# Linear attention and a GELU layer on one core: keys and values cut into 512 main tokens and 64 rest tokens, in place of nine tokens to a partition

## The chip, the core and the metric

The kernel runs on one core of one Trainium2 chip. TensorE (PE) multiplies matrices and writes to PSUM, eight banks of 2 KB per partition. VectorE (DVE), ScalarE (ACT) and GpSimd (POOL) do the elementwise work in SBUF, which has 128 partitions; DVE and ACT also read PSUM. SyncE (SP) only issues transfers (DMA); ACT issues some as well. Each engine takes its instructions in order, and they wait for one another through semaphores.

The metric is the time of one execution in microseconds (us), as the median of several. In the profile, L380 is line 380 of the kernel, and `out<-in` names the tiles that an instruction writes and reads.

## The reference

Eight batches of eight heads, 576 tokens (S) and 64 channels (D) go through linear attention with the feature map phi(x) = elu(x) + 1. The heads are put side by side to 512 channels, and a two-layer network follows: 512 to 2048 (`w_in`), GELU in its tanh form, 2048 to 512 (`w_out`). All is float32 in HBM.

```python
phi = lambda x: np.where(x > 0, x, np.exp(x) - 1.0) + 1.0
q_p, k_p = phi(q), phi(k)                            # q, k, v: (8, 8, 576, 64)
kv  = np.einsum('bhsd,bhse->bhde', k_p, v)           # 64 x 64 for each batch and head
z   = np.sum(k_p, axis=2)
num = np.einsum('bhsd,bhde->bhse', q_p, kv)
den = np.einsum('bhsd,bhd->bhs', q_p, z)[..., None] + 1e-06
x = (num / den).transpose(0, 2, 1, 3).reshape(8 * 576, 512)
h = x @ w_in                                         # (4608, 2048)
g = 0.5 * h * (1.0 + np.tanh(np.sqrt(2 / np.pi) * (h + 0.044715 * h**3)))
out = g @ w_out                                      # (4608, 512)
```

## The kernel before

**Feature map.** phi is computed as min(exp(x), max(x + 1, 1)). ACT takes the exponential (`exp_of`, L212), DVE takes max(x + 1, 1) (`linear_of`, L220) and then the minimum (`least_of`, L228). The results are bf16 (`q_p`, `k_p`).

**Queries.** Of each batch, tokens 0 to 511 (`MAIN`) are loaded with four tokens to a partition and all eight heads side by side (`load_q`, L99). The last 64 tokens (`REST`) of two batches share one tile of 128 partitions, `qr` (`load_rest`, L110). The minimum of q is transposed by four DMA transposes on SP's queue to `qt`, channels on the partitions (`least_q`, L597).

**Keys and values.** The 576 tokens of a head are 64 partitions of nine tokens each (J = 9), so two neighbouring heads, which lie one behind the other in HBM, fill 128 partitions: `load_pairs` (L90) reads runs of 2304 bytes, and four pairs of heads (`u`) make a tile. `v` is cast to bf16 into `vp`, which has a 65th column of ones for each head (E = 65), so that one product gives both kv and z.

**The kv products** (`kv_paired`, L242). For each of nine token slots, a pair of heads `u = 2 * ii + s` and a member `a` of the pair, a matmul contracts 64 partitions: the array is used as four quarters of 64x64. Row half `a` is the head within the pair, column half `s` the pair. A batch takes 9 x 2 x 2 x 2 = 72 matmuls of 64 columns by 65. The results go into block-diagonal tiles `kvbds` (a head pair in two 64x65 blocks, 128x130 in all) for batches 0 to 3, or compact tiles `kvs` for batches 4 to 7.

**The n products**, q_p times kv with the denominator as 65th column. For batches 0 to 3, `nab` (L311) and its kin use the block-diagonal tile: per 128 tokens four matmuls of 128x128 by 130 columns. For batches 4 to 7, `n_quads` (L276) uses quarters of 64x64: 16 matmuls by 65 columns per 128 tokens. `divide` (L289) is a reciprocal and a multiplication on DVE, which give `x`. `x` is transposed to `xt` by a DMA transpose on SP's queue (`transposed_x`, L621); for batches 0 and 1 PE transposes.

**The network.** `iteration(j)` (L741) runs the two large products for batch j's 512 tokens; iteration 8 does the rest tokens of all eight batches (`xt_rest`). It has 16 steps h (four matmuls of 512 columns each; ACT applies GELU into `g`) and 16 steps o (four matmuls each; four tiles t of 128 tokens by four ranges of m). From iteration 2 on all h come first (slots 0 to 15), then o by tiles (slots 16 to 31). Evictions of o alternate between DVE and ACT, and ACT issues the stores.

**The order by hand.** The schedule is manual. `at(j, slot, fn)` puts a piece of attention work for a later batch behind a slot of iteration j; work of one slot runs in the order in which it was registered. This order is also that of every queue, SP's among them:
- `plan_prepare(b, ...)` (L575): the maps of batch b and its cast of v; for b from 4 on in iteration b - 2 at slots 13 to 19.
- `plan_by_chunks` (L628): kv and the four chunks of n for batches 2 (iteration 1, slots 16 to 24) and 3 (iteration 2, slots 2 to 10).
- `plan_attention(b, m_rest)` (L636): for batches 4 to 7, in iteration b - 1, an early block at slot 5 (two chunks of n and the rest of two batches) and a late one at slot 22 (two chunks, kv of batch b + 1, the minimum and the transposes of q of batch b + 1).
- `load_batch` (L118): q, k and v of a batch on SP's queue; batch 2 before the first matmul of the network, batch 4 in iteration 1 at slot 29, 5 in iteration 2 at slot 23, 6 and 7 in iterations 3 and 4 at slot 6. k and q of batch 3 come with batch 2, its v and the first rest of q in iteration 1 at slot 10.

**Storage.** Loads go to seven buffers of one pool (`pld`), rests of q to two (`pqr`). In PSUM, six single banks rotate among h, o and the small products (`ps_b`), and one pair of banks (`ps_a`, `pair_of_banks`) serves n and kv.

**Batches 0 and 1** have their own paths (`first_batch`, `plan_second`) with PE transposes. SP loads them first, together with the weights, which DVE, ACT and POOL cast to bf16.

**The last tile** (`last_tile`, L733) of iteration 8 is computed in three pieces of columns; ACT copies the first, DVE the other two (L738).

Of the kernel before, what the change touches and what calls it, by code (L numbers as in the profile page):

```python
# [15 lines left out]
def kernel(  # L16
# [33 lines left out]
    pld = ctx.enter_context(tc.tile_pool(name="pld", bufs=7))  # L50
    pqr = ctx.enter_context(tc.tile_pool(name="pqr", bufs=2))
# [32 lines left out]
    ld = {}  # L84

    def ld_tile(name, b):
        shape = [P, H, C * D] if name == "q" else [P, NP, J * D]
        ld[name, b] = pld.tile(shape, FP32, name=name + "_x", tag="ld")
# [10 lines left out]
    def load_q(b):  # L99
        ld_tile("q", b)  # L100
        nc.sync.dma_start(
            out=ld["q", b],
            in_=q[b, :, 0:MAIN, :].rearrange("h (p c) d -> p h (c d)", c=C),
        )

    def load_all_pairs(name, src, b):
        ld_tile(name, b)
        load_pairs(name, src, b)

    def load_rest(m):  # L110
        t = ld["qr", m] = pqr.tile([P, H, D], FP32, name="qr")
        for s in range(2):
            nc.sync.dma_start(
                out=t[REST * s : REST * (s + 1)],
                in_=q[2 * m + s, :, MAIN:S, :].rearrange("h p d -> p h d"),
            )

    def load_batch(b):  # L118
        load_q(b)
        load_all_pairs("k", k, b)  # L120
        load_all_pairs("v", v, b)
# [53 lines left out]
    load_q(3)  # L175
    load_all_pairs("k", k, 3)
# [6 lines left out]
    vps = [pkv.tile([P, J * NP, E], BF16, name=f"vp{i}") for i in range(2)]  # L183
    kvbds = [pkv.tile([P, NP, 2 * E], BF16, name=f"kvbd{i}") for i in range(4)]
    kvs = [pkv.tile([P, NP, E], BF16, name=f"kv{i}") for i in range(4)]
    for i in range(2):
        nc.gpsimd.memset(vps[i][:, :, D:E], 1.0)
    for t in kvbds:
        nc.gpsimd.memset(t, 0.0)

    def vp_paired(b):
        return vps[b % 2].rearrange("p (j u) e -> p j u e", u=NP)

# [4 lines left out]
    def maps_view(name, b, x, out, hs):  # L198


        i = x[:, hs].rearrange("p h (c d) -> p h c d", d=D)
        o = out[:, :, hs, :].rearrange("p c h d -> p h c d")
        if name == "qr" or (name == "q" and b > 1):
            i = i.rearrange("p (u a) c d -> p a u c d", a=2)
            o = o.rearrange("p (a u) c d -> p a u c d", a=2)
        return o, i
# [5 lines left out]
    def exp_of(name, b, hs=None):  # L212
        x = ld[name, b]
        hs = hs or slice(0, x.shape[1])
        if (name, b) not in exps:
            exps[name, b] = pe.tile([P, x.shape[2] // D, x.shape[1], D], BF16, name=name + "_e")
        o, i = maps_view(name, b, x, exps[name, b], hs)
        nc.scalar.activation(o, i, AF.Exp)  # L218

    def linear_of(name, b, hs=None):  # L220
        x = ld[name, b]
        hs = hs or slice(0, x.shape[1])
        if (name, b) not in phi:
            phi_tiles(name, b)
        o, i = maps_view(name, b, x, phi[name, b], hs)
        nc.vector.tensor_scalar(o, i, 1.0, 1.0, op0=ALU.add, op1=ALU.max)  # L226
# [9 lines left out]
    def cast_v_paired(b, us, fn):  # L236
# [3 lines left out]
        )  # L240

# [14 lines left out]

    def kv_evac(b, blocks, src, fn):
        for s in range(2):
            r = slice(HP * s, HP * (s + 1))
            fn(out=kvbds[b][r, blocks, E * s : E * (s + 1)], in_=src[r])  # L260

    def nab_mm(qt_c, kvbd, ns):
        for i in range(NP):
            nc.tensor.matmul(  # L264
                ns[i // 2][:, 2 * E * (i % 2) : 2 * E * (i % 2 + 1)],
                lhsT=qt_c[:, i, :],
# [4 lines left out]
    def kv_of_head(b, s, i):  # L271

        r = slice(HP * s, HP * (s + 1))
        return kvs[b % 4][r, i, :] if b > 3 else kvbds[b][r, i, E * s : E * (s + 1)]

    def n_quads(qt_c, bs, ns):  # L276

        for i in range(NP):
            for t in range(2):
                for s in range(2):  # L280
                    c = slice(HP * t, HP * (t + 1))
                    nc.tensor.matmul(  # L282
                        ns[s][c, E * i : E * (i + 1)],
                        lhsT=qt_c[HP * s : HP * (s + 1), i, c],
                        rhs=kv_of_head(bs[t], s, i),
                        skip_group_check=True,
                    )

    def divide(x_v, n_v):  # L289

        heads = tuple(slice(None) for _ in n_v.shape[:-1])
        shape = list(n_v.shape[:-1])
        r = psm.tile(shape, FP32, name="r" + "".join(str(d) for d in shape[1:]))
        nc.vector.reciprocal(r, n_v[heads + (D,)])  # L294
        nc.vector.tensor_tensor(  # L295
            x_v,
            n_v[heads + (slice(0, D),)],
            r[heads + (None,)].to_broadcast(shape + [D]),
            op=ALU.mult,
        )  # L300

    def x_tile():
        return px.tile([P, d_model], BF16, name="x")

    def by_parity(x):
        return x.rearrange("p (u a d) -> p a u d", a=2, d=D)

    def by_half(x):
        return x.rearrange("p (i s a d) -> p s a i d", s=2, a=2, d=D)

    def nab(qt_c, b):  # L311
        x, n_ps = x_tile(), pair_of_banks("n_ps")
        nab_mm(qt_c, kvbds[b], [n_ps[:, a] for a in range(2)])
        divide(by_parity(x), n_ps[:, :, 0 : 4 * E].rearrange("p a (u e) -> p a u e", e=E))
        return x

    def nab_in_banks(qt_c, b):
        x, ns = x_tile(), [bank("n_ps", [P, 4 * E]) for _ in range(2)]
        nab_mm(qt_c, kvbds[b], ns)
        for a in range(2):  # L320
            divide(by_parity(x)[:, a], ns[a].rearrange("p (u e) -> p u e", e=E))
        return x

    def nab_quads(qt_c, bs):

        n_ps = pair_of_banks("n_ps")
        n_quads(qt_c, bs, [n_ps[:, s] for s in range(2)])

        def x_of():
            x = x_tile()  # L330
            n_v = n_ps[:, :, 0 : NP * E].rearrange("p s (a i e) -> p s a i e", a=2, e=E)
            divide(by_half(x), n_v)
            return x

        return x_of

    def nab_quads_in_banks(qt_c, bs):
        ns = [bank("n_ps", [P, NP * E]) for _ in range(2)]
        n_quads(qt_c, bs, ns)

        def x_of():
            x = x_tile()
            for s in range(2):
                divide(by_half(x)[:, s], ns[s].rearrange("p (a i e) -> p a i e", a=2, e=E))
            return x

        return x_of
# [59 lines left out]
    def first_batch():  # L407
# [50 lines left out]
        x = {0: x_tile()}  # L458
# [116 lines left out]
    def plan_prepare(b, s_linear, s_exp):  # L575
        def casts():
            cast_v_paired(b, slice(0, NP), nc.vector.tensor_copy)

        order = "qk" if b < 5 else "kq"

        def exps_all():
            for n in order:
                exp_of(n, b)

        j, s = s_linear
        for i, n in enumerate(order):
            at(j, s + i, linear_of, n, b)
# [3 lines left out]
        if b < 5:  # L591
            at(j, s + 2, least_q, b)
            at(j, s + 4, least_of, "k", b)
        else:
            at(j, s + 2, least_of, "k", b)

    def least_q(b):  # L597
        least_of("q", b)
        qts[b] = pt.tile([P, C, NP, P], BF16, name="qt")
        for c in range(C):  # L600
            nc.sync.dma_start_transpose(
                out=qts[b][:, c],
                in_=phi["q", b][:, c].rearrange("p h d -> p (h d)"),
            )

    def kv_in_pair(b):
        kv_ps = pair_of_banks("kv_ps")
        for ii in range(2):
            kv_paired(b, ii, lambda a, ii: kv_ps[:, a, E * ii : E * (ii + 1)])
        src = kv_ps[:, :, 0 : 2 * E].rearrange("p a (i e) -> p a i e", e=E)  # L610
        if b > 3:
            nc.vector.tensor_copy(out=kvs[b % 4].rearrange("p (a i) e -> p a i e", a=2), in_=src)
        else:
            for s in range(2):
                r = slice(HP * s, HP * (s + 1))
                nc.vector.tensor_copy(
                    out=kvbds[b][r, :, E * s : E * (s + 1)].rearrange("p (a i) e -> p a i e", a=2),
                    in_=src[r],
                )

    def transposed_x(b, c, x):  # L621
        if b not in xts:
            xts[b] = pt.tile([P, NP, MAIN], BF16, name="xt")
        nc.sync.dma_start_transpose(out=xt_chunk(b, c), in_=x)

    rest_qt = {}

    def plan_by_chunks(b, j, s_kv, s_n):  # L628
        def n(c):
            transposed_x(b, c, nab(qts[b][:, c], b))  # L630

        at(j, s_kv, kv_in_pair, b)
        for c in range(C):
            at(j, s_n + 2 * c, n, c)

    def plan_attention(b, m_rest):  # L636


        j = b - 1

        def pair_of_chunks(c):
# [193 lines left out]
```

## Time and profile before

| What | Value |
|---|---|
| Three runs | 287.03, 286.35, 285.89 us; median 286.35 |
| The profiled execution's own time | 287.03 us |
| Its span, first to last instruction | 285.2 us |
| Granted clock of TensorE | 1.00 |
| Large matmuls of 512 columns, L725 and L380 | 560 + 492 + 64, 379 ns each, starts 0.216 us apart |
| kv matmuls L248, 64 rows x 64 columns x 65 | 576, busy 6.6 us |
| n matmuls L264, 128 x 128 x 130 | 60, busy 5.8 us |
| n matmuls L282, 64 x 64 x 65 | 256 + 64, busy 4.9 us |
| Loads of k and v, 1152 KB each | median 10.8 and 11.8 us from issue to landing |
| Loads of q, 1024 KB each | 6.4 us |
| Loads of rests of q, 128 KB each | 9.0 us |
| DMA transposes of x | 24, 3.7 us |

Matmuls are pipelined: one of 512 columns is shown with 379 ns, but the next starts 216 ns after it, so the time of a stretch is read from starts, or from the chain of waits, and not from a sum of durations. Time of an engine other than PE counts only where PE waits for it. The chain of waits names, in order of time, the instructions that followed one another up to the end of the execution.

### The profile page before, as it was taken

The page shows a single profiled execution, that of the slowest core. Times are in us where ns is not written, and L with a number is a line of the kernel's source. Part 1 is how long each engine was busy: PE and PEld are TensorE (multiplying, and loading weights), DVE is VectorE, ACT ScalarE, POOL GpSimd, SP SyncE. Part 2 cuts the span into 40 slices and gives each one's busy share as a digit, 9 for nine tenths or more (in the row PEclk, how much of TensorE's full clock was granted, in tenths as well). Part 3 has the DMA queues.
Part 4 walks back from the last instruction along what each step waited for, and adds up shares of the span by engine and source line. Part 5 has one row for each costly group of instructions (what it writes and reads, how often), then busy time and mean ns, then how long its engine had stood idle before and what let it go on. Part 6 is the DMA issues. An engine that isn't in the chain of part 4 may idle for free.

```text
span 285.2 us, 5408 instructions
## 1 busy us (share of the span) xinstructions
PE 278.3 (98%) x2298; PEld 135.7 (48%) x2298; DVE 106.8 (37%) x192; ACT 161.2 (57%) x222; POOL 19.0 (7%) x24
## 2 busy tenths in 40 slices
PE   7999999999989999999999999999999999999995
PEld 3484455445445444445444544454444444444444
DVE  2850396434865550727072815372403000000001
ACT  4768876795966844684368626771650165026400
POOL 4147251000000000000000000000000000000000
PEclk9999999999999999999999999999999999999999
DMA  6999999926998958999828953006310610120022
GB/s 232 400 406 397 411 401 403 404 60 194 160 223 285 289 147 259 332 339 307 168 45 301 302 164 79 19 21 175 103 37 1 121 65 0 49 90 11 0 74 75
DMA packets 59575, 53.83 MB, mean 189 GB/s; under 512 B 35744, under 2 KB 45344, under 8 KB 59552
## 3 DMA queue, kind: packets, MB, share of 16 engines
q1 hardware_dynamic: 56768, 44.57, 52.2%
q10 hardware_dynamic: 2784, 8.91, 9.0%
q8 instruction: 18, 0.29, 0.4%
q14 instruction: 5, 0.04, 0.1%
HBM read 36.70 MB, written 9.44 MB: 162 GB/s over the span
## 4 chain that ended last, share of the span: by engine, by line
PE 82%; DMA 10%; DVE 3%; SPq 2%; issue 1%; POOL 1%; DVEq 0%
PE h_ps L380 39%; PE o_ps L725 39%; DMA w_st<-in_moe_w_in_dram 5%; DMA k_x<-in_k_dram 4%; PE kv_ps L248 2%; PE n_ps L282 1%; SPq L129 1%; PE n_ps L264 1%; DMA xt<-x 1%; SPq L92 1%; DVE k_p L232 1%; POOL w_in_sb L141 1%; DVE vp L237 1%; DVE q_p L232 0%; DVE q_p L226 0%
## 5 line engine op out<-in xcount | busy, mean ns | idle before, releaser
L725 PE MATMUL o_ps<-w_out_sb,g 128*128 128x512 bf16 (+2 forms) x608 | 127.9, 368 | 0.0
L380 PE MATMUL h_ps<-xt,w_in_sb 128*128 128x512 bf16 (+1 forms) x564 | 115.4, 360 | 0.7 <-DMA xt<-x 0.7
L390 ACT ACTIVATE g<-h_ps 128x512 bf16<-128x512 f32 x144 | 84.9, 599 | 42.0 <-PE h_ps L380 41.1
L380 PEld LDWEIGHTS <-w_in_sb 128*128 128x128 bf16 x628 | 57.8, 98 | 63.7 <-issue 1.4
L725 PEld LDWEIGHTS <-g 128*128 128x128 bf16 x608 | 57.6, 98 | 64.1
L686 ACT COPY o_sb<-o_ps 128x512 f32<-128x512 f32 (+1 forms) x19 | 10.8, 575 | 65.0 <-PE o_ps L725 64.1
L686 DVE COPY o_sb<-o_ps 128x512 f32<-128x512 f32 (+1 forms) x19 | 12.3, 647 | 73.5 <-PE o_ps L725 73.5
L295 DVE TENSOR_TENSOR x<-n_ps,r 128x256 bf16<-128x256 f32 (+1 forms) x49 | 26.4, 539 | 1.7
L294 DVE RECIPROCAL r<-n_ps 128x4 f32<-128x4 f32 (+1 forms) x49 | 9.2, 187 | 39.8 <-PE n_ps L282 30.1
L232 DVE TENSOR_TENSOR k_p<-k_p,k_e 128x2304 bf16<-128x2304 bf16 (+1 forms) x9 | 11.9, 1317 | 18.9 <-ACT k_e L218 18.8
L218 ACT ACTIVATE k_e<-k_x 128x2304 bf16<-128x2304 f32 (+1 forms) x9 | 17.1, 1904 | 0.9 <-DMA k_x<-in_k_dram 0.8
L218 ACT ACTIVATE q_e<-q_x 128x2048 bf16<-128x2048 f32 (+1 forms) x9 | 15.4, 1716 | 3.3 <-DMA q_x<-in_q_dram 3.2
L226 DVE TENSOR_SCALAR q_p<-q_x 128x2048 bf16<-128x2048 f32 (+1 forms) x9 | 9.9, 1103 | 13.7 <-DMA q_x<-in_q_dram 13.6
L380 PE MATMUL h_ps<-xt_rest,w_in_sb 128*128 128x512 bf16 x64 | 14.0, 379 | 0.0
L226 DVE TENSOR_SCALAR k_p<-k_x 128x2304 bf16<-128x2304 f32 (+1 forms) x9 | 11.0, 1222 | 6.2 <-DMA k_x<-in_k_dram 6.2
L232 DVE TENSOR_TENSOR q_p<-q_p,q_e 128x2048 bf16<-128x2048 bf16 (+1 forms) x9 | 9.9, 1101 | 7.3 <-ACT q_e L218 7.2
L237 DVE CAST vp<-v_x 128x2304 bf16<-128x2304 f32 (+1 forms) x9 | 11.4, 1266 | 2.3 <-DMA v_x<-in_v_dram 2.2
L412 PE MATMUL w_ps<-warm 128*128 128x512 bf16 x37 | 10.1, 423 | 1.2 <-DVE warm L181 1.2
L403 ACT ACT_TABLE_LOAD x8 | 10.3, 1283 | 0.1
L218 ACT ACT_TABLE_LOAD x7 | 9.0, 1283 | 0.1
L141 POOL CAST w_in_sb<-w_st 128x512 bf16<-128x512 f32 (+2 forms) x6 | 7.6, 1269 | 14.8 <-DMA w_st<-in_moe_w_in_dram 14.8
L147 POOL CAST w_out_sb<-w_st 128x2048 bf16<-128x2048 f32 (+2 forms) x5 | 7.1, 1427 | 8.7 <-DMA w_st<-in_moe_w_out_dram 8.7
(47 smaller groups left out, 76.8 us busy)
## 6 DMA issues: line engine op xcount, KB each, us to landing
out_dram<-o_sb ACTq DMA_DIRECT2D x16, 512.0 KB, 3.5
k_x<-in_k_dram SPq DMA_DIRECT2D x7, 1152.0 KB, 10.8
v_x<-in_v_dram SPq DMA_DIRECT2D x7, 1152.0 KB, 11.8
q_x<-in_q_dram SPq DMA_DIRECT2D x6, 1024.0 KB, 6.4
w_st<-in_moe_w_in_dram SPq DMA_DIRECT2D x3, 1024.0 KB, 13.6
w_st<-in_moe_w_out_dram SPq DMA_DIRECT2D x3, 1024.0 KB, 12.4
q_x<-in_q_dram SPq DMA_DIRECT2D x4, 512.0 KB, 8.5
k_x<-in_k_dram SPq DMA_DIRECT2D x2, 576.0 KB, 6.1
```

What stands on the lines that cost most here:

```text
L141: fn(out=w_in_sb[:, :, 512 * i + fs.start : 512 * i + fs.stop], in_=w_st[True, i][:, :, fs],)
L218: nc.scalar.activation(o, i, AF.Exp)
L226: nc.vector.tensor_scalar(o, i, 1.0, 1.0, op0=ALU.add, op1=ALU.max)
L232: nc.vector.tensor_tensor(p, p, e, op=ALU.min)
L237: fn(out=vp_paired(b)[:, :, us, 0:D].rearrange("p j u d -> p u j d"), in_=ld["v", b][:, us].rearrange("p u (j d) -> p u j d", d=D),)
L295: nc.vector.tensor_tensor(x_v, n_v[heads + (slice(0, D),)], r[heads + (None,)].to_broadcast(shape + [D]), op=ALU.mult,)
L380: nc.tensor.matmul(h_ps[:, ts], lhsT=w_in_sb[:, c, P * m : P * (m + 1)], rhs=xt[:, c, ts], start=(c == 0), stop=(c == KM - 1), skip_group_ ...
L390: nc.scalar.activation(g[:, m, :], h_ps, AF.Gelu_apprx_tanh)
L403: nc.scalar.preload_act_table_set("gelu_apprx_tanh_and_others")
L412: nc.tensor.matmul(w_ps, lhsT=warm[:, 0:P], rhs=warm)
L686: (nc.scalar.copy if on_scalar else nc.vector.tensor_copy)(dst, src)
L725: nc.tensor.matmul(o_ps, lhsT=g[:, m, P * t : P * (t + 1)], rhs=w_out_sb[:, m, fs], start=(m == 0), stop=(m == MM - 1),)
```

## The change

Batches 0 and 1 keep the layout with nine tokens to a partition (`PAIRED`). For batches 2 to 7 the following is changed.

- k and v are loaded as q is: 512 main tokens, four to a partition, runs of 1024 bytes (`load_main`). The last 64 tokens of two batches share a tile of 128 partitions, `kr` and `vr`, loaded in two transfers each by runs of 256 bytes, with the even batch and ahead of its v (`load_rest`).
- kv contracts 128 partitions: four chunks of main tokens and the rest, two heads side by side in the column halves, 40 matmuls per batch (`kv_main`). For the rest the other batch's rows of `vrs` are zero. All results go into the block-diagonal tiles, four in turn.
- n uses the block-diagonal tile in all batches: four matmuls by 130 columns per 128 tokens. The rest of q takes four such matmuls for each of two batches, with 64 columns each. `n_quads` and what calls it are gone.
- The order: kv at slot 2 of iteration b - 1, n at slots 4, 6, 8 and 10 for every batch from 3 on; the rest of q at slot 2 of iterations 3, 4, 5 and 7, ahead of kv. Batches 6 and 7 are loaded at slot 23 of iterations 3 and 4. The first rest of q is loaded in four transfers (by parity of the head) in place of two; the later ones move to slot 18 of iterations 1, 3 and 5.
- The maps of an even batch take in kr (exp, linear step, minimum) and two casts of vr; q's channels are no longer reordered by parity in the maps.
- POOL sets two further tiles to zero, with columns of ones in their own rows. One pool, `prest`, is new and holds kr and vr.

```diff
+    prest = ctx.enter_context(tc.tile_pool(name="prest", bufs=1))
...
+    PAIRED = (0, 1)
 
     def ld_tile(name, b):
-        shape = [P, H, C * D] if name == "q" else [P, NP, J * D]
+        shape = [P, NP, J * D] if b in PAIRED and name != "q" else [P, H, C * D]
         ld[name, b] = pld.tile(shape, FP32, name=name + "_x", tag="ld")
...
-    def load_rest(m):
-        t = ld["qr", m] = pqr.tile([P, H, D], FP32, name="qr")
+    def load_main(name, src, b):
+        ld_tile(name, b)
+        nc.sync.dma_start(
+            out=ld[name, b],
+            in_=src[b, :, 0:MAIN, :].rearrange("h (p c) d -> p h (c d)", c=C),
+        )
+
+    def load_rest(name, src, m):
+        t = (pqr if name == "qr" else prest).tile([P, H, D], FP32, name=name)
+        ld[name, m] = t
         for s in range(2):
-            nc.sync.dma_start(
-                out=t[REST * s : REST * (s + 1)],
-                in_=q[2 * m + s, :, MAIN:S, :].rearrange("h p d -> p h d"),
-            )
+            r = t[REST * s : REST * (s + 1)]
+            rows = src[2 * m + s, :, MAIN:S, :]
+            if name == "qr" and m == 0:
+                for a in range(2):
+                    nc.sync.dma_start(
+                        out=r[:, NP * a : NP * (a + 1), :],
+                        in_=rows.rearrange("(u a) p d -> p a u d", a=2)[:, a],
+                    )
+            else:
+                nc.sync.dma_start(out=r, in_=rows.rearrange("h p d -> p h d"))
 
     def load_batch(b):
-        load_q(b)
-        load_all_pairs("k", k, b)
-        load_all_pairs("v", v, b)
+        load_main("q", q, b)
+        load_main("k", k, b)
+        if b % 2 == 0:
+            load_rest("kr", k, b // 2)
+            load_rest("vr", v, b // 2)
+        load_main("v", v, b)
...
+    vrs = [pkv.tile([P, H, E], BF16, name=f"vr{s}") for s in range(2)]
...
+        nc.gpsimd.memset(vrs[s], 0.0)
+        nc.gpsimd.memset(vrs[s][REST * s : REST * (s + 1), :, D:E], 1.0)
...
+    def cast_vr(m):
+        for s in range(2):
+            r = slice(REST * s, REST * (s + 1))
+            nc.vector.tensor_copy(out=vrs[s][r, :, 0:D], in_=ld["vr", m][r])
...
+    def kv_main(b, i, kv_ps):
+        kp, vp = phi["k", b], vp_main(b)
+        kr, vr = phi["kr", b // 2], vrs[b % 2]
+        for c in range(C + 1):
+            for s in range(2):
+                h = 2 * i + s
+                nc.tensor.matmul(
+                    kv_ps[HP * s : HP * (s + 1), i, :],
+                    lhsT=kp[:, c, h, :] if c < C else kr[:, 0, h, :],
+                    rhs=vp[:, c, h, :] if c < C else vr[:, h, :],
+                    start=(c == 0),
+                    stop=(c == C),
+                    skip_group_check=True,
+                )
...
-    def nab_mm(qt_c, kvbd, ns):
+    def nab_mm(qt_c, kvbd, ns, rows=slice(0, P)):
         for i in range(NP):
             nc.tensor.matmul(
-                ns[i // 2][:, 2 * E * (i % 2) : 2 * E * (i % 2 + 1)],
-                lhsT=qt_c[:, i, :],
+                ns[i // 2][rows, 2 * E * (i % 2) : 2 * E * (i % 2 + 1)],
+                lhsT=qt_c[:, i, rows],
                 rhs=kvbd[:, i, :],
                 skip_group_check=True,
             )
...
+    def plan_attention(b, j, s_kv, s_n):
+        def kv():
+            if j == 1:
+                kv_ps = pair_of_banks("kv_ps")[:, 0, 0 : NP * E].rearrange("p (i e) -> p i e", e=E)
+            else:
+                kv_ps = bank("kv_ps", [P, NP, E])
+            for i in range(NP):
+                kv_main(b, i, kv_ps)
+            kv_evac(b, slice(0, NP), kv_ps, nc.vector.tensor_copy)
+
+        def n(c):
+            x = nab(qts[b][:, c], b)
+            if c == 0:
+                xts[b] = pt.tile([P, NP, MAIN], BF16, name="xt")
+            nc.sync.dma_start_transpose(out=xt_chunk(b, c), in_=x)
+
+        at(j, s_kv, kv)
         for c in range(C):
...
+            at(j, s_n[c], n, c)
+
+    def plan_rest(m, j, s_exp, s_least, j_n):
...
+        def n():
+            n_ps = pair_of_banks("n_ps")
+            for s in range(2):
+                nab_mm(
+                    box["qt"],
+                    kvbds[(2 * m + s) % 4],
+                    [n_ps[:, a] for a in range(2)],
+                    slice(REST * s, REST * (s + 1)),
+                )
+            x = nab_evac(n_ps, 2 * m in PAIRED)
+            nc.sync.dma_start_transpose(out=xt_rest[:, :, P * m : P * (m + 1)], in_=x)
...
-    plan_by_chunks(2, 1, 16, 18)
-    plan_by_chunks(3, 2, 2, 4)
-    at(1, 10, load_all_pairs, "v", v, 3)
-    at(1, 10, load_rest, 0)
-    at(1, 18, load_rest, 1)
+    plan_attention(2, 1, 16, (18, 20, 22, 24))
+    at(1, 10, load_main, "v", v, 3)
+    at(1, 10, load_rest, "qr", q, 0)
+    at(1, 29, load_batch, 4)
     plan_prepare(3, (1, 24), (1, 23))
-    plan_rest(0, 1, 23, 1, 28)
+    plan_rest(0, 1, 23, 28, 3)
     at(1, 23, gelu_table)
-    at(1, 29, load_batch, 4)
-    at(3, 2, kv_in_pair, 4)
     for b in range(4, B):
         plan_prepare(b, (b - 2, 13), (b - 2, 15))
-    for b in range(4, B):
-        plan_attention(b, {4: 0, 5: 1, 6: 2, 7: 3}.get(b))
-    at(2, 23, load_batch, 5)
-    at(3, 6, load_batch, 6)
-    at(4, 6, load_batch, 7)
-    at(3, 6, load_rest, 2)
-    at(4, 6, load_rest, 3)
-    for m, j in ((1, 2), (2, 4), (3, 5)):
-        plan_rest(m, j, 15, j, 22)
+        if b > 4:
+            at(b - 3, 23, load_batch, b)
+    for m in range(1, 4):
+        at(2 * m - 1, 18, load_rest, "qr", q, m)
+        plan_rest(m, 2 * m, 15, 22, (4, 5, 7)[m - 1])
     for b in range(4, B):
         at(b - 2, 15, gelu_table)
+    for b in range(3, B):
+        plan_attention(b, b - 1, 2, (4, 6, 8, 10))
```

## The prediction

> **What bounds the kernel now.** I read the page's engine shares first, then its forty slices, then the waits of TensorE (PE), then the chain of waits in order of time.
>
> ```profile
> PE 278.3 (98%) x2298; PEld 135.7 (48%) x2298; DVE 106.8 (37%) x192; ACT 161.2 (57%) x222; POOL 19.0 (7%) x24
> ...
> PE   7999999999989999999999999999999999999995
> ...
> DMA  6999999926998958999828953006310610120022
> ```
>
> PE works in all but 7 of 285 us, and apart from the first slice, the last and one of 8 its row is full; VectorE (DVE) and ScalarE (ACT) have room. DMA is full for 57 us and then in bursts.
>
> ```profile
> PE w_ps L412 <- DVE warm L181: 1.2, 1, 1.2
> PE h_ps L380 <- DMA xt<-x: 0.7, 1, 0.7
> PE kv_ps L248 <- DVE vp L237: 0.7, 1, 0.7
> PE t_ps L422 <- DVE q_p L232: 0.5, 2, 0.3
> ```
>
> These are all of PE's waits but one of 0.2 us. Three lie in the first 41 us, in batches 0 and 1, whose path the diff leaves alone. The second, 0.7 us at 79 us, is the first matmul of iteration 2, held by the last transpose of batch 2's x. So from 41 us to the end the time is the sum of PE's instructions plus that wait, and the change is to be priced in small matmuls. The chain of waits shows each (start us, length us, what):
>
> ```profile
> 63.75 0.71 PE kv_ps L248 x72
> 64.46 1.83 PE h_ps L380 x8
> 66.29 0.23 PE n_ps L264 x4
> 66.52 1.73 PE h_ps L380 x8
> ...
> 114.71 0.54 PE n_ps L282 x48
> 115.25 8.74 PE h_ps L380 x40
> ...
> 130.03 0.38 PE n_ps L282 x32
> 130.41 0.67 PE kv_ps L248 x72
> 131.09 7.88 PE o_ps L725 x36
> ```
>
> Eight large matmuls cost 1.73 behind four full-array n matmuls, but 1.83 behind a block of 64x64 matmuls: such a block costs 0.10 more than its own line says (40 cost 8.74 where 40 x 0.216 = 8.64).
>
> **PE, the kv products of batches 2 to 7.** Before, 72 matmuls of 64 rows by 64 columns, four at a time. Alone (batches 2, 3, 4) they cost 0.71 + 0.10 = 0.81 or 0.82, together 2.45. Beside the late n block (batches 5 to 7) they cost 0.67 each, since entry and exit are shared: 2.01. Sum 4.46.
>
> After, 40 matmuls of 128 rows by 64 columns, two at a time, in a block of their own for every batch. No row has that shape. The timeline gives the nearest one:
>
> ```profile
> 111.24 0.78 PE L248 MATMUL kv_ps<-vp,k_p 64*64 64x65 bf16 x72
> ```
>
> With the last matmul's own 0.195 (the mean of its row) taken off, 72 starts spread over 0.585, so a group of four follows the last after 0.585/17.75 = 0.033. The rest of the 0.81, 0.22, is entering and leaving. In those 0.033 the left and right column halves both get a matmul of 65 columns on the same rows, so halves run together; I take 0.033 for a pair too: 19.5 x 0.033 + 0.22 = 0.86, six times 5.16, **+0.7**. Lower end: starts are limited by count (0.585/71 = 0.0082 each), 39 x 0.0082 + 0.22 = 0.54, six times 3.24, -1.2. Upper end: halves follow one another at 0.033, 39 x 0.033 + 0.22 = 1.51, six times 9.06, +4.6.
>
> A rule speaks against the change here. The Trainium skill, TensorE: Matmul & The Clock Gate, section LDWEIGHTS, gives a weight load the number of columns over 1.2 in ns, and TensorEngine Tiling (Array Packing), Restrictions and Gotchas, says that column tiling excludes the fast load. Forty loads of 64 columns that nothing overlaps would be an estimated 2.1 us per batch, and the change some 8 us more. The same trace has 72 loads of 64 columns in 0.67 us, so I go by the row.
>
> **PE, the n products of batches 4 to 7.** Before: early blocks of two chunks and the rest 0.54 + 0.10 = 0.64, late blocks of two chunks 0.38 + 0.11 = 0.49; four of each, 4.52. After: 16 chunks of four full-array matmuls at 0.23 = 3.68, as batches 2 and 3 have them already. The four rest blocks are eight matmuls of 64 columns by 130; the row that is nearest is n's 130 at 0.23/4 = 0.058. The loop does four on one half, then four on the other, so I take them one after another, 8 x 0.058 = 0.46; lower end 0.23, if halves overlap. Three stand directly before a kv block in slot 2 and share its entry, the last pays 0.22: 4 x 0.46 + 0.22 = 2.06 (lower 1.14). Together 5.74 against 4.52, **+1.2** (lower +0.3).
>
> **The SyncE (SP) queue and the wait at 79 us.** Every load and every x transpose goes through it.
>
> ```profile
> 66.47 0.53 SPq L92 DMA_DIRECT2D v_x<-in_v_dram  x1
> 67.04 2.27 SPq L113 DMA_DIRECT2D qr<-in_q_dram  x2
> 69.43 1.24 SPq L624 DMA_TRANSPOSE xt<-x  x1
> 70.71 3.24 SPq L113 DMA_DIRECT2D qr<-in_q_dram  x2
> 74.05 3.88 SPq L624 DMA_TRANSPOSE xt<-x  x3
> ```
>
> The four x of batch 2 are ready on DVE at 67.5, 69.5, 71.4 and 73.4; the last three transposes go out at 74.05 to 77.9, one every 1.3 us, because two rest loads hold the queue until 74. The last lands at 79.03 and PE waits 0.72 for it. After, the first rest load is issued in four parts in place of two, ahead of all four transposes. Issues of this line took 0.60 to 2.59, median 1.12 in this stretch. Where they are long the queue is backed up, since v landed at 74.15 and the rest loads by 74.5, 74.9, 76.3 and 76.7; two more issues of the same bytes are then partly absorbed. Lower end -0.7 (the wait goes), upper +2.2 (two issues at 1.12 all late). I take **+0.2**. The 0.05 by which kv of batch 2 delays PE only shortens this wait.
>
> The other added issues: kr and vr bring four DMAs with batches 2, 4 and 6, ahead of v.
> - Batch 2: SP is at them near 39 us, its loads land one per 2.7 to 2.9 us, and two rest loads behind a v landed 0.3 and 0.7 later than it. v of batch 2 (landed at 51.1) comes some 2 us later, and DVE, done with k's linear step at 51.8, waits about 1 us. What is queued behind the cast is q's minimum, which waits for exp until 59.8. Hidden; the slack is 6 us.
> - Batch 4: issued between 86 and 88 us, ahead of batch 3's four x transposes, which landed at 101.2 and are wanted at 108.6. Four issues at 1.1 make 4.5 us late, 2.9 left. The v cast on DVE (97.65, already waiting for its landing) moves to about 100, q's minimum and its transposes to 104 and 109; PE wants them from 113 on. Behind that cast DVE also holds the eviction of output tile 0 until about 104; its bank is wanted at 110. If the cover is gone, each us goes straight to PE.
> - Batch 6 moves to iteration 3, slot 23, some 25 us before use; batch 7 likewise a stage later. Their rows landed within 12 us.
>
> **DVE, ACT, POOL: nothing.** 2048 columns in place of 2304 save 0.53 per batch on DVE (1.36 to 1.22, 1.48 to 1.22, 1.36 to 1.22); per even batch, 512-column steps for kr (0.42 and 0.43) and two casts of vr (at most 0.42 each) add 1.7. ACT saves 0.2 per batch and adds 0.61 per even one. Net about +1.9 and +0.7 under an otherwise saturated PE. The tightest place is kv of batch 2: kr's minimum should end near 63.4, kv starts at 63.7. POOL's memsets ended by 3.5 us, its next work starts at 13.5; two more of 0.53 and two small ones fit. The single n accumulator is refilled every second slot (1.73 of PE work plus); DVE empties it in 0.21 + 0.69, as in batches 2 and 3, where PE never waited. In slot 2, the rest's 0.9 and kv's 0.87 end some 0.5 before n of chunk 0 starts.
>
> **Sum.** 0.7 + 1.2 + 0.2 = +2.1 us; all lower ends -1.6, all upper ends +8.0. The profiled execution took 287.03 around a span of 285.2; it would become 289.1 around 287.3. It was the slowest of the three, 0.68 over the median of 286.35, so I add to the median: **288.4**.
>
> **Rivals.**
> 1. Column halves do not overlap when all 128 rows are in use: kv 1.51 in place of 0.86, +3.9, **292.3**. It decides from 0.045 a pair. For: no such row here. Against: in the groups of four, halves already share rows. Chance 0.08.
> 2. The transposes on SP become the limit: the split rest load before iteration 2, or kr and vr before iteration 3, delay x by two issues more, +2.0, **290.4**. For: iteration 2 already waits and SP shows its backlog. Against: 7 us of slack at iteration 3. It decides from an x landing later than 79.9 or 109. Chance 0.15.
> 3. Not slower: small matmuls cost by count, 0.0082 a start. Then 40 in place of 72 save 0.32 per batch against my 0.86, -1.9 in all, **286.5**. For: starts inside a group of four are only some ns apart, and the later groups are evenly filled. Against: four matmuls that overlap fully would still need 65 columns' time, which is near 0.033. It decides below 0.025 a pair. Chance 0.20.
> 4. The change does not do what its words say: every tile that it adds is 2048 or 1024 bytes per partition, so what follows moves by multiples of 512, and DVE copies the last piece already (L738). Layout then changes nothing and only the sum above remains; no price of its own, chance 0.05 that it moves something unseen.
>
> **How the numbers follow.** The forecast has 0.52, its own range is 287.4 to 289.6. The range of 286.7 to 291.0 leaves out rival 1, part of 3, and the tails. A measurement of this kernel (285.89 to 287.03) can tell about 0.5%, 1.4 us, from no change: faster would be under 284.9, slower over 287.8. Faster needs rival 3 and the wait at 79 us gone: 0.06. Same is most of rival 3, rival 4 and the forecast's lower edge: 0.31. Slower 0.63.
>
> **What would show it.** In the chain after: six kv lines of 40 matmuls near 0.76 each with 0.10 behind; n lines of four at 0.23 in iterations 3 to 6; rest blocks near 0.46; the wait for x at iteration 2 between 0.5 and 1.5, none at iteration 3. A kv line of 1.4 is rival 1, of 0.45 rival 3; a new PE wait for xt is rival 2. The prediction is wrong if PE shows a wait in slots 2 to 10 for the n accumulator, or a change in the first 41 us.

## The result, and the profile after

The changed kernel takes 287.47 us, the median of six runs (287.03 to 287.91); the kernel before took 286.16 us beside it (six runs, 285.89 to 287.03). The ratio (here and below not that of the two medians) is 1.0041, with a 95% interval of 1.0024 to 1.0059: 0.7 to 1.7 us slower. That is clear of noise but under the half per cent that the prediction had named as its bound, so by that bound it counts as no change. The profiled execution took 287.54 us around a span of 285.7. In a few single executions of the versions below, three of the six of the layout alone among them, the granted clock was 0.988 to 0.994 in place of 0.997 to 1.000, and all of these but one took 1.5 to 5.9 us more than the median of the others of their version.

The engine shares and slices of the page after:

```profile
PE 279.5 (98%) x1882; PEld 137.6 (48%) x1882; DVE 108.6 (38%) x181; ACT 163.8 (57%) x227; POOL 20.2 (7%) x28
...
PE   8999999999999999999999999999999999999994
...
DMA  7999998987979948935896489535121210120022
```

PE has 416 matmuls fewer and is busy 1.2 us longer; DVE works 1.8 us more (1.9 was expected) and ACT 2.6 (0.7 was expected; 1.3 of it is an eighth load of a table for the exponential), and neither shows in PE's waits. The waits of PE after:

```profile
PE w_ps L413 <- DVE warm L189: 1.2, 1, 1.2
PE kv_ps L275 <- DVE vp L253: 0.7, 1, 0.7
PE n_ps L354 <- ACT kvbd L302: 0.2, 1, 0.2
PE t_ps L423 <- DVE q_p L248: 0.2, 1, 0.2
```

The wait for x at iteration 2 is no longer among them. The chain of waits has the new small blocks, the short runs of kv and n matmuls between the large ones (start us, length us, what): kv of batch 2 alone, n of one chunk, rest and kv in one block, kv of batch 7 alone, the last rest alone.

```profile
63.43 0.76 PE kv_ps L290 x40
64.19 1.83 PE h_ps L381 x8
66.02 0.23 PE n_ps L306 x4
...
110.45 0.36 PE n_ps L306 x8
110.81 0.64 PE kv_ps L290 x40
111.45 1.83 PE h_ps L381 x8
...
199.45 0.76 PE kv_ps L290 x40
...
228.87 0.37 PE n_ps L306 x8
```

From here on a block's cost is taken more finely than the chain's two digits allow: from the start of the large matmul ahead of the block to the start of the one behind it, less the 0.216 us that large matmuls stand apart anyway. Such sums from 60 us on agree within 0.02 us between executions of one kernel.

| us on PE, from 60 us on | Before | After |
|---|---|---|
| kv of batches 2 to 7 | 2.43 alone, 2.02 beside n | 6 x 0.852 = 5.11 |
| n of batches 4 to 7 | 8 blocks x 0.474 = 3.79 | 16 x 0.236 = 3.78 |
| n of batches 2 and 3 | 8 x 0.235 = 1.88 | 8 x 0.236 = 1.89 |
| four rest blocks | 4 x 0.157 = 0.63 | 3 x 0.245 + 0.461 = 1.20 |
| Sum | 10.75 | 11.97 |

The difference is 1.22 us, against a measured 1.31. The two profiled executions stand only 0.5 us apart in span because that of the kernel before was the slowest of its six runs: it had the wait at iteration 2, and the first matmul of iteration 2 started 1.10 us after its predecessor in place of 0.47 after the change. Whether that wait belongs to the kernel or to the execution was the open question.

### The profile page after: what moved, and what is told of

Same layout as the page of the kernel before. It is cut to its first block, busy times and chain, and to the rows that moved or that the text cites. A ratio compares the mean times of both kernels' runs of the same rounds, so it can differ in the third digit from the quotient of the medians.

```text
span 285.7 us, 4612 instructions
## 1 busy us (share of the span) xinstructions
PE 279.5 (98%) x1882; PEld 137.6 (48%) x1882; DVE 108.6 (38%) x181; ACT 163.8 (57%) x227; POOL 20.2 (7%) x28
## 4 chain that ended last, share of the span: by engine, by line
PE 84%; DMA 9%; SPq 2%; DVE 2%; issue 1%; POOL 1%
PE o_ps L705 41%; PE h_ps L381 39%; DMA w_st<-in_moe_w_in_dram 5%; DMA k_x<-in_k_dram 4%; PE n_ps L306 3%; PE kv_ps L290 1%; SPq L137 1%; DVE k_p L248 1%; SPq L94 1%; POOL w_in_sb L149 1%; DVE vp L253 1%; SPq L99 0%; PE t_ps L373 0%; PE kv_ps L275 0%; DVE o_sb L666 0%
## 5 line engine op out<-in xcount | busy, mean ns | idle before, releaser
L381 PE MATMUL h_ps<-xt,w_in_sb 128*128 128x512 bf16 (+1 forms) x564 | 118.0, 360 | 0.1
L319 DVE RECIPROCAL r<-n_ps 128x8 f32<-128x8 f32 x33 | 6.8, 207 | 49.0 <-PE n_ps L306 49.0
L321 DVE TENSOR_TENSOR x<-n_ps,r 128x512 bf16<-128x512 f32 x33 | 22.8, 691 | 1.1
L224 ACT ACTIVATE k_e<-k_x 128x2048 bf16<-128x2048 f32 (+2 forms) x9 | 15.8, 1758 | 0.9 <-DMA k_x<-in_k_dram 0.8
L306 PEld LDWEIGHTS <-qt 128*128 128x128 bf16 x124 | 9.5, 98 | 6.1
L235 DVE TENSOR_SCALAR k_p<-k_x 128x2048 bf16<-128x2048 f32 (+2 forms) x9 | 10.2, 1133 | 5.4 <-DMA k_x<-in_k_dram 5.4
L306 PE MATMUL n_ps<-kvbd,qt 128*128 128x130 bf16 x124 | 12.1, 221 | 0.0
L413 PE MATMUL w_ps<-warm 128*128 128x512 bf16 x37 | 10.2, 424 | 1.2 <-DVE warm L189 1.2
L248 DVE TENSOR_TENSOR k_p<-k_p,k_e 128x2048 bf16<-128x2048 bf16 (+2 forms) x9 | 11.0, 1228 | 0.8 <-ACT k_e L224 0.6
L259 DVE CAST vp<-v_x 128x2048 bf16<-128x2048 f32 x6 | 7.4, 1226 | 5.7 <-DMA v_x<-in_v_dram 5.7
```

Source lines behind the costliest of these rows:

```text
L224: nc.scalar.activation(by_chunk(exps[name, b], hs), x[:, hs].rearrange("p h (c d) -> p h c d", d=D), AF.Exp,)
L235: nc.vector.tensor_scalar(by_chunk(phi[name, b], hs), x[:, hs].rearrange("p h (c d) -> p h c d", d=D), 1.0, 1.0, op0=ALU.add, op1=ALU.max,)
L248: nc.vector.tensor_tensor(p, p, e, op=ALU.min)
L259: fn(out=vp_main(b)[:, :, :, 0:D].rearrange("p c h d -> p h c d"), in_=ld["v", b].rearrange("p h (c d) -> p h c d", d=D),)
L306: nc.tensor.matmul(ns[i // 2][rows, 2 * E * (i % 2) : 2 * E * (i % 2 + 1)], lhsT=qt_c[:, i, rows], rhs=kvbd[:, i, :], skip_group_check=True,)
L321: nc.vector.tensor_tensor(x_view(x, paired), n_v[:, :, :, 0:D], r[:, :, :, None].to_broadcast([P, 2, NP, D]), op=ALU.mult,)
```

## The experiments

Theory A: the change costs the sum of PE's small blocks, and the wait at iteration 2 is variation between executions. Theory B: the change lengthens the blocks and, through the queue, shortens that wait. Each run stands beside runs of the kernel before on the same chip.

**The kernel before, profiled again.** No edit.

> The kernel before, profiled once more. Theory A (the change costs only the sum of PE's small blocks; what else differs between the two profiles is variation between executions): the small blocks from 60 us on again add 10.75 us, and the wait for x at iteration 2, 0.72 us in the first profile, is anywhere from 0 to 0.9. Theory B (the change also shortens that wait, by about 0.6 us, through the queue): the wait is again 0.6 to 0.9.

The span was 284.1 and the time 285.85. The waits of PE in that execution are these:

```profile
PE w_ps L412 <- DVE warm L181: 1.2, 1, 1.2
PE kv_ps L248 <- DVE vp L237: 0.2, 1, 0.2
PE n_ps L353 <- ACT kvbd L260: 0.2, 1, 0.2
```

The wait for x is gone with nothing changed: the first matmul of iteration 2 followed after 0.27 us. The wait for vp near 40 us, in the part that the diff leaves alone, fell from 0.7 to 0.2. The blocks sum to 10.73. On SP's queue the same transfers as before, from the load of v on, were quicker by 0.8 us:

```profile
65.94 0.53 SPq L92 DMA_DIRECT2D v_x<-in_v_dram  x1
66.51 1.48 SPq L113 DMA_DIRECT2D qr<-in_q_dram  x2
68.09 2.03 SPq L624 DMA_TRANSPOSE xt<-x  x1
70.17 2.43 SPq L113 DMA_DIRECT2D qr<-in_q_dram  x2
72.69 3.88 SPq L624 DMA_TRANSPOSE xt<-x  x3
```

The last three transposes leave from 72.69 on, in place of 74.05. That is 1.36 us earlier, while PE itself was only 0.53 earlier (kv of batch 2 started at 63.15 in place of 63.68); the 0.83 between the two is what the wait lost. Theory A stands, and so does the lesson that a wait of 0.7 us in one profile may be one execution's.

**The second rest load of q out of the transposes' way.**

```diff
-    at(1, 18, load_rest, 1)
+    at(2, 2, load_rest, 1)
```

> Before, with the second rest load of q moved from iteration 1, slot 18, to iteration 2, slot 2, so that the last three x transposes of batch 2 need not wait behind it. If the wait at iteration 2 is a steady part of before: it goes, 0.6 to 0.7 us less, 285.5. If it is not: no difference, 286.2, and the wait is as small in before profiled again.

285.87 us against 286.14, ratio 1.0001 (0.9973 to 1.0028): no difference that can be measured, as is to be expected of a wait that is mostly absent. The interval reaches 0.8 us to either side, so the time alone does not exclude the 0.6 to 0.7 of the first expectation; what speaks against a steady wait is the profile of the kernel before, taken again. It was the one version that might have beaten both kernels, and it is not shown to.

**The n part and the order alone.** k and v stay nine tokens to a partition; kv stays 72 matmuls, but in a block of its own in slot 2; n uses the block-diagonal tile everywhere.

```diff
-    for b in range(4, B):
-        plan_attention(b, {4: 0, 5: 1, 6: 2, 7: 3}.get(b))
...
+        at(2 * m - 1, 18, load_rest, m)
+        plan_rest(m, 2 * m, 15, 2 * m, 22, (4, 5, 7)[m - 1])
...
+    for b in range(3, B):
+        plan_by_chunks(b, b - 1, 2, 4)
```

> The n part and the order alone, k and v as before. Theory A: 24 chunks of n at 0.236 (5.7), six kv blocks of 72 at 0.81 (4.9), rest blocks 0.25 three times and 0.46 once (1.2): 11.7 in place of 10.75, so 0.95 us over before, 287.1. If going from 64 columns on 128 rows to 64 on 64 rows drains the array too, 0.15 more for each of three blocks, 287.5. Theory B: the wait at iteration 2 stays near 0.7, since v of batch 3 is loaded as before.

287.18 us against 286.14, ratio 1.0033 (1.0012 to 1.0053). The blocks sum to 12.05, 1.30 more than before, between the two figures expected and near the upper one: rest and kv together cost 1.170, where rest 0.245 and kv 0.804 would make 1.05, so going from one tiling of the array to another costs 0.12. PE shows no wait at iteration 2, with v loaded as before. This part alone loses as much as the whole change. Of its 1.30, 0.36 are the three changes of tiling, which the changed kernel does not have; in their place it has 0.28 for kv's new shape (below). So in the new order the layout of k and v costs PE nothing: 11.97 against 12.05.

**The layout of k and v alone.** The loads, maps and kv of the changed kernel, in the order of before, with n in quarters.

```diff
-                kv_ps = [bank("kv_ps", [P, 2, E]) for _ in range(2)]
-                for ii in range(2):
-                    kv_paired(b + 1, ii, lambda a, ii: kv_ps[a][:, ii, :])
+                kv_ps = bank("kv_ps", [P, NP, E])
+                kv_main(b + 1, kv_ps)
```

> The layout of k and v alone (main and rest, 40 matmuls per kv), n in quarters and in the order of before. Theory A: three kv blocks at 0.85, three beside late n blocks at 0.65 more, early and late blocks as before: 10.7 to 11.2 in place of 10.75, so 286.2 to 286.7. Theory B: the wait at iteration 2 is 0.3 or less, v of batch 3 lands some 1.5 us earlier, and the time is 285.6 to 286.1.

289.62 us against 286.14, ratio 1.0111 (1.0073 to 1.0150). Neither theory had this. The blocks sum to 11.31, 0.57 over before. Of that, 0.17 is a wait inside one block, for the transposed rest of q (`qtr`, landed at 175.45; the block at 175 took 0.80 in place of 0.63); the 11.14 without it lie in the expected 10.7 to 11.2. The bulk is a new wait, of 1.8 us at the start of iteration 4. The chain of waits through it (`issue` is time in which the engine waited for nothing that the profile shows):

```profile
130.61 4.44 PE o_ps L770 x20
135.04 0.02 issue
135.07 0.62 DVE o_sb L731
135.69 4.44 DMA xt<-x
140.13 0.14 issue
140.26 5.34 PE h_ps L418 x24
```

The timeline of SP's queue ahead of it (start us, time that the issue takes, line, tiles, count):

```profile
121.05 0.57 SPq L102 DMA_DIRECT2D q_x<-in_q_dram  x1
121.71 0.75 SPq L102 DMA_DIRECT2D k_x<-in_k_dram  x1
122.55 4.05 SPq L110 DMA_DIRECT2D kr<-in_k_dram  x2
126.66 2.59 SPq L110 DMA_DIRECT2D vr<-in_v_dram  x2
129.29 0.99 SPq L102 DMA_DIRECT2D v_x<-in_v_dram  x1
130.32 1.79 SPq L110 DMA_DIRECT2D qr<-in_q_dram  x2
132.21 4.69 SPq L671 DMA_TRANSPOSE xt<-x  x2
```

kr and vr hold the queue for 6.6 us. They stand ahead of the late transposes of batch 4's x, which land at 139.65 and 140.13 and release PE. Before has the same place in the order with q, k, v and qr, but no kr or vr: there the two landed by 136.6, ahead of iteration 4 at 139. The first of them left only 0.7 us later than before (132.21 against 131.55). What came late was its landing: in both kernels it landed about half a microsecond behind the last load ahead of it, and that load landed at 139.18 in place of 134.32. The wait (1.94 from start to start) and the blocks make 2.5 us; the execution profiled here took 288.94, 2.8 over before.

**The same, with batches 6 and 7 loaded behind those transposes.**

```diff
-    at(3, 6, load_batch, 6)
-    at(4, 6, load_batch, 7)
+    at(3, 23, load_batch, 6)
+    at(4, 23, load_batch, 7)
```

> The layout of k and v alone, as in k_alone, but batches 6 and 7 loaded at slot 23 of iterations 3 and 4, behind the late x transposes, in place of slot 6. If the 1.9 us that k_alone waited at iteration 4 come from the seven transfers ahead of those transposes on SP's queue: the wait goes, and with small blocks of 11.3 against 10.75 the time is 0.6 over before, 286.7. If it is something else of the layout (DVE's longer maps, for one): the wait stays, 288.5 to 289.6.

287.55 us against 285.92, ratio 1.0050 (1.0024 to 1.0076). The wait for x at iteration 4 is gone, so its cause was the order on the queue. The time is 0.85 over what was expected. Of the two waits of PE below, the first is that of the start, which executions of the kernel before show with 0.2 to 0.7 as well. The second is new: v of batch 6 lands only at 155.78, its cast on DVE stands ahead of k's minimum, and so the minimum is late for kv in iteration 4, by 0.8 us from start to start. A block of iteration 5 waits 0.3 more for `qtr`. With both, the blocks sum to 12.22, 1.5 over before, and that covers the excess.

```profile
PE kv_ps L281 <- DVE vp L241: 0.6, 1, 0.6
PE kv_ps L266 <- DVE k_p L236: 0.5, 1, 0.5
```

With the order of before, neither of the two places for the loads lets the layout go free.

**The order of before's loads in the changed kernel.**

```diff
-            at(b - 3, 23, load_batch, b)
+            at(b - 3, 23 if b == 5 else 6, load_batch, b)
```

> The changed kernel with batches 6 and 7 loaded at slot 6 of iterations 3 and 4, as before has them. If the change's order (all n by slot 10) is what keeps its loads harmless: x transposes of batches 4 and 5 land some 6 us later, still ahead of their iterations, and the time stays 287.5. If the layout's longer queue costs wherever loads stand before transposes: a wait at iteration 4 as in k_alone, 1 to 2 us more, 288.5 to 289.5.

289.23 us against 285.92, ratio 1.0116 (1.0075 to 1.0157); the blocks sum to 11.97 as in the changed kernel. The first expectation fell: even with n done by slot 10, three transposes behind the rest loads landed too late for iteration 4, as the chain of waits shows.

```profile
124.88 8.01 PE o_ps L705 x38
132.89 5.58 DMA xt<-x
138.47 0.14 issue
138.61 2.75 PE h_ps L381 x12
```

So it is the place of the loads, slot 23, that keeps the longer queue harmless in the changed kernel, together with transposes that are on their way by then.

**kv twice.**

```diff
-        for c in range(C + 1):
+        for c in [*range(C + 1)] * 2:
```

> The changed kernel with every kv product computed twice (80 matmuls per batch, same result); the rest's two halves stand on two lines of the source, in the same order. Theory A: what PE does in these blocks goes to the end one for one. 40 more starts at 0.0163 are 0.65 per batch, 3.9 us in all: 291.4, 5.2 over before. Theory C (PE has hidden slack in slots 2 to 10, so that its sum counts only in part): less than 2 us over the changed kernel, 289.5 or less. The rest: in program order, one half's four matmuls start before the other half's; if the array runs the halves in pairs all the same, starts of the two lines alternate.

290.70 us against 285.92, ratio 1.0162 (1.0139 to 1.0186), 4.0 to 5.3 us over before. The blocks sum to 15.80, 3.83 over the changed kernel's (0.639 per batch for 40 matmuls). The expected 5.2 lies in the interval and theory C's 2 us over the changed kernel does not fit: what these blocks take goes to the end nearly one for one (3.5 of 3.83 us, each kernel against its own runs of before). The two lines of the rest show something else. The timeline of PE:

```profile
111.14 0.24 PE L652 MATMUL n_ps<-kvbd,qtr 128*64 128x130 bf16 x1
111.15 0.24 PE L659 MATMUL n_ps<-kvbd,qtr 128*64 128x130 bf16 x1
111.22 0.22 PE L652 MATMUL n_ps<-kvbd,qtr 128*64 128x130 bf16 x1
111.23 0.22 PE L659 MATMUL n_ps<-kvbd,qtr 128*64 128x130 bf16 x1
111.28 0.22 PE L652 MATMUL n_ps<-kvbd,qtr 128*64 128x130 bf16 x1
```

In the program, in PE's list of instructions as in the source, all four matmuls of L652 come ahead of all four of L659. In the profile they start by turns, 0.013 apart, a pair every 0.06.

**Two more rest loads with each even batch,** into tiles that nothing reads.

```diff
+            for _ in range(2):
+                load_rest("kr", k, b // 2, True)
```

> The changed kernel with two more rest loads of k (four transfers) with each even batch, into tiles that nothing reads. Theory A with the slack of 7 us at iteration 3: SP is some 4 us later, the last x transpose of batch 3 lands near 105 in place of 100.6, PE does not wait, 287.5. Theory D (the queue is at its limit): a wait for xt or qt in iteration 3, 1 to 3 us more, 288.5 to 290.5.

291.70 us against 285.92, ratio 1.0205 (1.0180 to 1.0230). Both expectations named iteration 3; PE waited in iteration 1. v of batch 2 landed at 60.0 in place of 53.4, and its cast on DVE held back q's minimum, so that q's transposes left 2.6 us late (63.40 against 60.84). They landed 6.0 late (69.39 against 63.42), behind k of batch 3, which had left SP at 60.15 and landed at 68.82; why SP stood for 9 us ahead of batch 3's loads was not tried. The chain of waits:

```profile
62.52 0.88 PE h_ps L387 x4
63.40 0.00 issue
63.40 5.99 DMA qt<-q_p
69.39 0.05 issue
69.43 0.41 PE n_ps L312 x4
```

That is the cover of batch 2, and how far it reaches: v some 2 us later than before costs nothing, and in this version another 6.6 us, with the later loads of batch 3, cost 3.1 in two waits (1.1 for k_p and 2.0 for qt; 3.6 from start to start).

**The same from batch 4 on.**

```diff
-            for _ in range(2):
+            for _ in range(2 if b > 2 else 0):
```

> As rests_twice, but the spare rest loads come with batches 4 and 6 alone. rests_twice spent the cover of batch 2 in iteration 1 (v landed 6.7 us later, past the 6 us that DVE had), so it did not test iteration 3 by itself. If iteration 3 has 7 us and four transfers cost up to 8 there: a wait for xt at iteration 3 of 0 to 1 us, 287.5 to 288.5. If the queue is at its limit in every stage (theory D): 2 us or more, 289.5.

287.42 us against 286.07, ratio 1.0051 (1.0038 to 1.0064): the time of the changed kernel. The last x of batch 3 landed at 106.2 in place of 100.6, and iteration 3 began at 107.5 without a wait. The slack there is real: 5.6 us of it were used, and 1.3 were left. Theory D, a limit in every stage, falls.

**The changed kernel once more.** No edit.

> The changed kernel, profiled and timed once more. Theory A: its small blocks add 11.97 us again, as each does in every execution; the wait at iteration 2 is anywhere from 0 to 0.9; 1.2 us over before, 287.3.

287.28 us against 286.07, ratio 1.0043 (1.0027 to 1.0060). The blocks sum to 11.97. This execution's span is 285.5, that of the kernel before, profiled again, 284.1: of the 1.4 us between them, 1.23 are the blocks, 0.39 a longer wait near 40 us, and -0.23 two smaller waits of the kernel before (0.05 at iteration 2 and 0.20 at iteration 4, less 0.03).

## Why the prediction was right, and where it was off

**The direction and what decides it: right.** The end is the sum of PE's instructions. Blocks of 10.75, 11.97, 12.05 and 15.80 gave 286.2, 287.5, 287.2 and 290.7 us, where the queue added no steady wait. kv twice shows it by more than the noise. The size is another matter: 287.47 lies within the forecast's own range of 287.4 to 289.6 by 0.07 us alone.

**kv: right.** 0.852 per batch against 0.86, 5.11 against 5.16. Two halves on all 128 rows overlap as the groups of four did: rival 1 would have shown 1.41 in the chain, rival 3 0.44, and it shows 0.76 where kv stands alone (0.64 behind a rest). By the price of a weight load that the Trainium skill gives (TensorE: Matmul & The Clock Gate, section LDWEIGHTS), an estimated 2.1 us would go to forty loads of 64 columns one after another. Here the forty matmuls, each with its load, start within 0.63, so the row that was set against that price decided rightly. Of kv's +0.66, 0.28 are the shape (0.852 against 0.805) and 0.39 that it no longer shares a block with n.

**n of the chunks: right.** 3.78 against 3.68, and nothing over the quarters' 3.79.

**The rest blocks: the term that was mis-sized.** The prediction took eight matmuls one after another, 0.46, because the loop does one half first, and had 2.06 in all. They cost 0.245 beside kv and 0.461 alone, 1.20 in all, close to its lower end of 1.14, since the halves run by turns in spite of that order, as the two lines in kv twice show. With 1.20 the prediction's sum on PE would have been 1.1 in place of 1.9; the blocks measured +1.22.

**The wait at 79 us: taken for steady, and it is not.** +0.2 was allowed around it, with -0.7 as the lower end. It was 0.89 over the usual distance in one execution of the kernel before, 0.05 in another, 0.26 and 0.03 in two of the kernel after. The split rest load cost SP 2.61 for four issues against 2.27 for two, and no wait follows from it. The two errors, 0.9 on the rests and 0.2 here, less 0.2 by which the chunks and the blocks of before were read too close to the chain's two digits, are the distance from 2.1 to the 1.2 of the blocks (1.3 in the medians). They also moved the outcome across the bound: the forecast said slower by over 0.5% with 0.63, and the ratio of 1.0041 lies in the 0.31 that it gave to no change.

**The covers.** Batch 2's was right: v landed at 53.4 (2.3 us later), and DVE waited 1.7 for it, unseen by PE. For batch 3, whose x waits behind the loads of batch 4, the transposes were expected 4.5 us late and landed at 100.6 against 101.2. kr and vr do stand ahead of them, and the first left SP at 92.9 in place of 87.5; but the four then took SP 6.0 us to issue in place of 10.2. In both kernels they landed behind v of batch 4, and that landed only 1.0 later (98.6 against 97.6). The slack of 7 us was right. Rival 2 did not happen, yet its mechanism is in the kernel: with the loads at slot 6 it costs 1.6 us at iteration 4. The move of batches 6 and 7 to slot 23, which the prediction passed over in a sentence, is what kept it out.

**Not settled.** What makes the waits near 40 us and 79 us differ between executions was not tried. Why matmuls of the two halves start by turns against the order of the program is not shown either, only that they do. A block in which rest, kv and n share one entry, in one tiling, was not built either.

## What to carry to other kernels

Where one engine is busy to the end, price a change in that engine's small blocks, with entry and exit, from the chain of waits; rows read to a tenth of a microsecond gave kv and the n of the chunks here to 0.1 us each in sum, and the miss was a shape that no row had, the rests. Profile the kernel before twice, ahead of counting a wait of half a microsecond as something to win or lose. A layout that needs more and smaller transfers was cheap on the engines here, but it needed a place in the queue where nothing urgent stands behind it, and that place has to be looked for together with the layout.

## What the runs showed of the hardware

- Matmuls on the two column halves of the array started by turns in kv twice, although the program has four for one half ahead of four for the other: a pair every 0.060 us with 130 columns. With 65 columns (kv, whose program takes the halves in turn) a pair came every 0.033.
- A block of tiled matmuls costs entry and exit: the first starts 0.309 after the large one ahead of it (0.216 otherwise) and the next large one 0.119 to 0.130 behind the last of 65 columns (0.154 behind a last one of 130, and 0.059 behind full-array matmuls of 130). Going from one tiling to another inside a block costs about 0.1: the next start came 0.120 after the last in the layout alone, where 0.023 pass between n and kv in the kernel before; and 0.150 in the n part alone, where 0.047 pass between rest and kv in the changed kernel.
- The same loads and transposes on SP's queue took 0.8 us more or less from one execution to the next: the last three transposes of batch 2 left 7.58 and 6.75 us after the load of v ahead of them in two executions of the kernel before.
- What a transpose on SP's queue took to land depended on the loads ahead of it. In iteration 3 it landed 0.5 us behind the last of them in the layout alone, 7.4 after its issue, and 0.6 behind the last in the kernel before, 3.4 after its issue.
